# Attention and routed feed-forward on one core: nine idle products instead of eleven, the last spread's halves swapped, some 35 table entries set otherwise

## The chip, the cores and the metric

The kernel runs on 1 core of one Trainium2 chip. The metric is the device time of one execution in microseconds (us), as the median of the runs timed. A core has five engines with an instruction queue each: PE (TensorE, matmuls; PEld is its loading of weights), DVE (VectorE), ACT (ScalarE), POOL (GpSimd) and SP (SyncE, which here only issues DMAs). They run beside one another and wait for each other by semaphores. L723 is line 723 of the kernel before; in the changed kernel the same line stands some 10 to 30 lines further down.

## The reference

Eight batches of S = 3136 tokens, D = 256, scores from a 64-wide `z` of which one array is both query and key. Attention with a squared ReLU in place of a softmax, a product with `u`, then a routed feed-forward for the 128 tokens of each batch with the largest gate score:

```python
scores = (1.0 / S) * np.matmul(z, z.transpose(0, 2, 1))      # symmetric
out = u * np.matmul(np.maximum(scores, 0.0) ** 2, v)
# routed part, per batch b, x = out
top = 128 tokens with the largest x[b] @ w_gate
ye = np.maximum(x[b, top] @ w1, 0.0) @ w2
out[b, top] += sigmoid(score)[:, None] * ye
```

## The kernel before, in words

**Tiles.** The query tokens of a batch come in 7 chunks: five of 512, one of 256, one of 320. For a chunk the 24.5 key tiles of 128 tokens come as 12 pairs and a single half tile (`Vr`), so 13 slots a chunk, 91 a batch, 728 in all. Slots are counted from 0 in each batch. A slot adds its keys' part to the chunk's four PSUM accumulators (`acc`). As the score matrix is symmetric, a block of squared scores that an earlier chunk has computed is written to DRAM (`squares<-aT`) and fetched back (`qk<-squares`): such a slot is "old" and needs no score products.

**A new slot.** PE computes the scores in three products of a high and a low part (`sc<-Z,ZH`, `sc<-Zl,ZH`, `sc<-Z,ZL`, L588; each part is two instructions, one for each half of the rows). There is one score buffer, so the next slot's scores wait until ACT has read it: `a<-sc` is the ReLU (L593). Then ACT takes the square's rounded part, `hi<-a` (L602); the full square `a<-a` is made on ACT (L609) or DVE (L613); the rest `lo<-a,hi` by DVE or POOL (both L694). PE then does 16 instructions with `hi` and 8 with `lo` (`acc<-hi,V`, `acc<-lo,V`, L723). DVE transposes the square for the DRAM copy (`aT<-a`, L656). An old slot has only `hi<-qk` (ACT, L551) and `lo<-qk,hi` (L694). Inputs are split in the same way: `ZH`, `Z`, `V` are casts (L183), `ZL`, `Zl` and V's low part differences (L184).

**Order.** The program is written in a fixed order; each engine runs its own part of it in that order. In slot k the scores of slot k+3 are issued in the middle of slot k's products (`more_scores`). Loads and casts of later data stand in a table of due slots (`plan`), and are issued ahead of a slot's products. The steps of choosing tokens and of the feed-forward are queues of small tasks, woven in one at a time. Which engine does a step is decided by a running account of each engine's work (`busy`, `spend`), unless the table `PICK` has an entry for that slot: `pick(kind, k, default)` (L485) reads `PICK[kind]` at 0 for the first batch, 1 for the six in the middle, 2 for the last. Kinds are `sq` (True: the square on ACT), `lo` (True: the difference on DVE), `tl` (True: a slot's transposes behind its difference), `ne` and `fa` (whether a slot takes a routing task).

**A chunk's end.** `finish_early` (L806) scales two accumulators by ACT (`x<-acc`, L813); `finish` (L817) adds the other two and multiplies by `u` on DVE (`acc<-acc,x` L826, `ut<-acc,ut` L827, half 1 ahead of half 0), DVE transposes to the output's layout (`x<-ut`, L836), POOL multiplies by the gate's weights (`ut<-x,w_run`, L845) and DVE adds up (`gate<-ut`, L854). For the last chunk of the last batch the gate score is a product on PE instead: `spread` (L914) takes half 0 and then half 1 of `ut`, two instructions each.

**The beginning.** `warm(11)` (L1716) issues eleven products of a tile of zeros while the first `z` is on its way; `start` (L1718) then writes the first three slots' steps out by hand.

Of the kernel before, what the change touches and what calls it, by code (L numbers as in the profile page):

```python
# [18 lines left out]
P = 128  # L19
# [10 lines left out]
BITS = 4  # L30
INT_MIN = -(1 << 31)
PICK = {
    "fa": {
        1: {19: False},
        2: {28: False, 30: False, 32: False},
    },
# [4 lines left out]
    },  # L41
    "ne": {
        0: {15: False, 17: True},
        1: {4: True, 13: True, 40: True, 41: False, 42: True, 65: False, 70: False, 71: True, 79: True, 83: False},
    },
# [4 lines left out]
    },  # L50
    "tl": {
        0: {4: True, 8: True, 10: True, 15: True, 50: True},
        1: {6: True, 7: True, 8: True, 26: True, 31: True, 46: True, 56: True},
        2: {0: True, 8: True, 9: False},
    },
}
VH = [0, 0, 0, 0, 0, 0, 0, 1, 0, 0, 1, 0, 1]
VP = [0, 0, 0, 0, 0, 0, -1, 0, 1, 1, 0, 0, -1]
VD = [1, 0, 0, 0, 0, 0, 0, 0, 0, 0, 0, 0, 0]
# [62 lines left out]
def attention_then_routed_ffn(ctx: ExitStack, tc: tile.TileContext, zt, ut, v, wg, w1, w2, cst, cst16, keys, outs, at, cap):  # L122
# [58 lines left out]
    def split(src, hi, lo, hi_on=None, lo_on=None):  # L181

        (hi_on or nc.scalar.copy)(hi, src)  # L183
        (lo_on or nc.vector.tensor_tensor)(lo, src, hi.bitcast(F32), op=ALU.subtract)  # L184
# [161 lines left out]
    def prep_z(b, i, of=None, on=None, hi_on=None):  # L346

        of = i if of is None else of
        a, n = part(i)
        o = a - part(of)[0]  # L350
        on = on or (nc.gpsimd.tensor_tensor if b else None)
        if i < WHOLE:
            for q in range(2):
                src = of_tokens(staged["z", b, of][:, o : o + CH], q)
                split(src, in_pairs(ZH, i, q), in_pairs(ZL, i, q), hi_on, lo_on=on)
            spend(act=0.1, pool=1.8 if b else 0.0)
            return
        m = min(n, NJ * P - a)
        src = staged["z", b, of][:, o : o + m].rearrange("p (f t a) -> p f t a", f=GT, a=Q)
        split(src, by_rows(ZHe, a, m), by_rows(ZLe, a, m), hi_on, lo_on=on)  # L360
        if m < n:
            single = slice(a + m - WIDE, a + n - WIDE)
            split(staged["z", b, of][:, o + m : o + n], ZHe[:, single], ZLe[:, single], lo_on=on)
        spend(pool=0.65 + 0.0017 * n if b else 0.0)
# [9 lines left out]
    def bring_z(b, c):  # L374

        c0, w = CHUNKS[c]
        t, tl = (const.tile([P, CH], F32R, name=name, tag=name, bufs=2)[:, within(c)] for name in ("Z", "Zl"))
        Z[b, c] = t, tl
        if c < WHOLE:
            st = staged.pop(("m", b, c)) if b or c else staged["z", 0, 0]  # L380
            on_dve = not (b or c) or busy["pool"] + 1.2 > busy["dve"] + 0.6
            split(st, t, tl, lo_on=nc.vector.tensor_tensor if on_dve else nc.gpsimd.tensor_tensor)
            spend(act=0.6, **{"dve" if on_dve else "pool": 0.6 if on_dve else 1.2})
            return
        m = min(w, NJ * P - c0)
        for z, to in ((ZHe, t), (ZLe, tl)):
            nc.scalar.copy(to[:, :m].rearrange("p (f t a) -> p f t a", f=GT, a=Q), by_rows(z, c0, m).bitcast(F32))
            if m < w:
                nc.scalar.copy(to[:, m:], z[:, c0 - WIDE + m : c0 - WIDE + w].bitcast(F32))
            spend(act=0.1 + 0.001 * w)  # L390

    def stage_v(b, g, queues=(nc.sync,) * GT):
# [17 lines left out]
    def prep_v(b, g, on=None, hi_on=None):  # L410

        st = staged["v", b, g // 2][:, g % 2 * 2 :]
        n = 2 if 2 * g < NJ else 1
        if n == 2:
            t = vpool.tile([P, 2, NK, 2 * P], F32R, name="V", tag="V")
        else:
            t = vpool.tile([P, 2, NK, P], F32R, name="Vr", tag="Vr", bufs=1)
        src = st[:, :n].rearrange("p a d -> p (a d)").rearrange("p (f h i) -> p h f i", h=NK, i=Q)
        parts_of = [t[:, w].rearrange("p h (f i) -> p h f i", i=Q) for w in range(2)]
        hi_on = hi_on or on  # L420
        lo_on, took = on or nc.gpsimd, {"dve": 1.0} if on else {"pool": 2.3} if hi_on else {"act": 0.6, "pool": 1.3}
        if not on and b == 0 and n == 2 and busy["pool"] + 1.3 > busy["dve"] + 0.6:
            lo_on, took = nc.vector, {"act": 0.6, "dve": 0.6}
        if b and VD[g]:
            lo_on, took = nc.vector, {"act": 0.6, "dve": 0.6}
        if b and VH[g]:
            hi_on = nc.vector
            took = {**took, "act": 0.0, "dve": took.get("dve", 0.0) + 0.6}
        split(src, *parts_of, hi_on and hi_on.tensor_copy, lo_on.tensor_tensor)
        for q in range(n):  # L430
            V[b, 2 * g + q] = t[:, :, :, q * P : (q + 1) * P]
        spend(**took)
# [63 lines left out]
    def spend(act=0.0, dve=0.0, pool=0.0):  # L496
        busy["act"] += act
        busy["dve"] += dve
        busy["pool"] += pool

    fetched = {}
    shared = {}
    stores = []
# [302 lines left out]
    def finish_early(b, c):  # L806

        w = CHUNKS[c][1]
        x = tail.tile([P, CH // Q, NK, Q], F32, name="x", tag="x", bufs=1)
        flat = x.rearrange("p f h r -> p (f h r)")  # L810
        sums = [flat[:, h * w : (h + 1) * w] for h in range(NK)]
        for h in range(NK):
            nc.scalar.mul(sums[h], acc[b, c][h][h], SCALE * SCALE)  # L813
        spend(act=0.3 + 0.0016 * w)
        early[b, c] = x, sums

    def finish(b, c):  # L817
# [72 lines left out]
    def scores_of(b, c, xT):  # L890
# [17 lines left out]
        def spread(h):  # L908
            if not bank:
                bank.append(acc_bank("spread")[:, :w])  # L910
            if more:
                nc.tensor.matmul(bank[0], consts["ones"], row[:, P:], start=True, stop=True)
            else:
                nc.tensor.matmul(bank[0], by_half[h].broadcast_to([P, P]), xT[:, h, :w], start=h == 0, stop=h == NK - 1)  # L914

        def seen(q):
            if q == 0:
# [9 lines left out]
                )  # L927
            spend(act=0.25, dve=0.45)

        return [lambda h=h: spread(h) for h in range(1 if more else NK)], seen  # L930


    def route(b):
# [742 lines left out]
    def more_scores(upto):  # L1676
        nonlocal issued
        while issued <= min(upto, len(slots) - 1):
            scores(issued)
            issued += 1  # L1680

    def settle_scores():
        square_scores()
        for x in lows:
            low(*x)
        lows.clear()
# [30 lines left out]

    def start():  # L1718
        stage_z(0, 0, queues=(nc.sync, nc.scalar))
        warm(11)  # L1720
        first = moe.tile([P, 1], F32, name="g", tag="g", bufs=2)
        nc.scalar.copy(first, idle[0][:, :1])
        stage_z(0, 1, (WHOLE - 1) * CH, CH)
        stage_v(0, 0, (nc.scalar, nc.scalar, nc.sync, nc.sync))
        stage_v(0, 1)
        more_z(0, 2, 1)
        more_z(0, 3, 1)
        low_parts = []
        prep_z(0, 0, None, lambda *x, **how: low_parts.append(lambda: nc.vector.tensor_tensor(*x, **how)), nc.vector.tensor_copy)
        bring_z(0, 0)  # L1730
        for fn in low_parts:
            fn()
        prep_z(0, 1, hi_on=nc.vector.tensor_copy)
        more_scores(0)
        prep_v(0, 0, nc.vector)
        busy["pool"] = 99.0
        settle_scores()
        more_scores(1)
        prep_v(0, 1)
        square_scores()  # L1740
        prep_z(0, 2, 1)
        settle_scores()
        prep_v(0, 2, hi_on=nc.gpsimd)
        more_scores(2)
        settle_scores()
        prep_v(0, 3, hi_on=nc.gpsimd)
        settle_turns()
        busy["pool"] = 0.0
        stage_v(0, 2)
        stage_v(0, 3)  # L1750
# [5 lines left out]
    clock = dve_at = ready = told = 0.0  # L1756
    held_posts = []
    for k, (b, c, js, is_old) in enumerate(slots):
        if k == 0:
            start()  # L1760
        for fn, act, dve in plan.get(k, ()):
            fn()
            spend(act, dve)
        tasks = []
# [38 lines left out]
            for op in f0[0][0][:3]:  # L1803
                op()
        within_end[0] = k % SLOTS >= SLOTS - 2
        mix(k, [op for ops, _ in tasks for op in ops], lambda: more_scores(k + LEAD))
        settle_turns()
        if len(js) == 1 and c == WHOLE:
            lows[0][-1]()
# [92 lines left out]
```

## Time and profile before

| | |
|---|---|
| timed, median of 3 runs | 2007.01 us (2005.39 to 2007.15) |
| the profiled execution's own time | 2004.37 us |
| its span, from first to last record | 2002.6 us |
| TensorE clock granted, mean | 0.998 |
| busy, share of the span | PE 99%, PEld 87%, ACT 75%, DVE 73%, POOL 64% |

How to read it: PE's share of the span is close to all of it, and PE is on the chain that ended last for 93% of its length. So the time is the sum of PE's instructions and of the pieces in which PE waits or its products run further apart than they could. The other engines have a quarter of their time free over the whole, but not everywhere: in the first 50 us ACT and DVE are nearly full. The rows below are of single places.

### The profile page before, as it was taken

Reading aid. Unit: us, or ns where it says so; the run is one execution under the profiler, and the core shown is the slowest. Engines: PE = TensorE matmul, PEld = TensorE weight load, DVE = VectorE, ACT = ScalarE, POOL = GpSimd, SP = SyncE. Lnnn points to the kernel's source line nnn. Section 1 sums busy time; section 2 is a strip of 40 time slices with the busy share of each in tenths; the row PEclk is TensorE's granted clock in tenths of the full one; section 3 lists DMA queues with packets and bytes.
Section 4 is the critical chain, followed back from the end, with each engine's and each line's share of the span. In section 5 each row is a group of like instructions: output and inputs, shape, how many; then the busy total and the mean of one; then the engine's idle time right before and its main releaser. Section 6 shows DMA issues by size and latency. Waiting matters only on the chain.

```text
span 2002.6 us, 51589 instructions
## 1 busy us (share of the span) xinstructions
PE 1981.1 (99%) x19969; PEld 1732.7 (87%) x19969; DVE 1464.4 (73%) x2719; ACT 1495.6 (75%) x2036; POOL 1289.9 (64%) x719
## 2 busy tenths in 40 slices
PE   9999999999999999999999999999999999999998
PEld 6788989899888998889988899888988889878787
DVE  8866688855898568874688746887478864876775
ACT  8786688766887578866798757887588776877653
POOL 4665468657776577755787467865677657775642
PEclk9999999999999999999999999999999999999999
DMA  6788768896678967788677886779867787667852
GB/s 196 224 248 229 227 192 241 237 259 193 199 220 237 241 195 213 216 233 242 185 226 213 235 227 201 221 204 241 237 203 221 200 206 218 199 186 188 230 152 90
DMA packets 450869, 426.96 MB, mean 213 GB/s; under 512 B 136576, under 2 KB 377792, under 8 KB 447808
## 3 DMA queue, kind: packets, MB, share of 16 engines
q1 hardware_dynamic: 449488, 421.18, 74.1%
q8 instruction: 156, 2.56, 0.6%
q0 software_dynamic: 768, 2.10, 0.3%
q14 instruction: 89, 0.73, 0.1%
q10 hardware_dynamic: 368, 0.39, 0.1%
HBM read 248.94 MB, written 174.60 MB: 211 GB/s over the span
## 4 chain that ended last, share of the span: by engine, by line
PE 93%; DMA 2%; ACT 2%; issue 1%; DVE 1%; SPq 0%; POOL 0%; POOLq 0%; ACTq 0%; DVEq 0%
PE acc L723 79%; PE sc L588 10%; PE h L1494 1%; PE sc L571 1%; ACT a L593 1%; DMA qk<-squares 1%; PE y L1550 1%; DMA vst<-in_v 1%; DMA wl<-w1l_there 1%; ACT hi L602 0%; POOL lo L694 0%; PE idle L1716 0%; DVE lo L694 0%; ACT x L813 0%; ACT hi L551 0%
## 5 line engine op out<-in xcount | busy, mean ns | idle before, releaser
L723 PE MATMUL acc<-hi,V 64*128 64x512 f32 (+2 forms) x10752 | 1238.2, 361 | 1.7 <-DVE ut L827 1.3
L723 PEld LDWEIGHTS acc<-hi,V 64*128 64x128 f32 x10752 | 976.3, 184 | 125.6 <-issue 5.5
L694 POOL TENSOR_TENSOR lo<-a,hi 128x1024 fp32r<-128x1024 f32 (+2 forms) x243 | 548.8, 2265 | 330.1 <-ACT a L609 236.6
L723 PE MATMUL acc<-lo,V 64*128 64x512 f32 (+2 forms) x5376 | 693.7, 360 | 2.5 <-POOL lo L694 2.1
L723 PEld LDWEIGHTS acc<-lo,V 64*128 64x128 f32 x5376 | 500.3, 184 | 63.2 <-POOL lo L694 6.2
L593 ACT ACTIVATE a<-sc 128x1024 f32<-128x1024 f32 (+2 forms) x345 | 327.0, 948 | 208.7 <-PE sc L588 196.5
L656 DVE STREAM_TRANSPOSE aT<-a 128x512 f32<-128x512 f32 (+1 forms) x494 | 315.8, 679 | 108.4 <-ACT a L609 100.6
L694 POOL TENSOR_TENSOR lo<-qk,hi 128x1024 fp32r<-128x1024 f32 (+2 forms) x156 | 309.3, 1991 | 101.4 <-ACT hi L551 56.0
L551 ACT CAST hi<-qk 128x1024 fp32r<-128x1024 f32 (+2 forms) x327 | 278.6, 855 | 123.0 <-PE acc L723 83.8
L602 ACT ACTIVATE hi<-a 128x1024 fp32r<-128x1024 f32 (+2 forms) x345 | 339.9, 985 | 24.7 <-PE acc L723 5.8
L609 ACT ACTIVATE a<-a 128x1024 f32<-128x1024 f32 (+1 forms) x280 | 279.2, 997 | 8.2
L694 DVE TENSOR_TENSOR lo<-qk,hi 128x1024 fp32r<-128x1024 f32 (+2 forms) x171 | 235.1, 1387 | 60.0 <-ACT hi L551 54.9
L694 DVE TENSOR_TENSOR lo<-a,hi 128x1024 fp32r<-128x1024 f32 (+1 forms) x102 | 133.2, 1306 | 54.5 <-ACT a L609 43.8
L184 POOL TENSOR_TENSOR V<-vst,V 128x512 fp32r<-128x512 f32 x85 | 138.4, 1634 | 48.9 <-ACT V L183 43.5
L845 POOL TENSOR_TENSOR ut<-x,w_run 128x1024 f32<-128x1024 f32 (+2 forms) x52 | 126.0, 2424 | 28.5 <-DVE x L836 17.0
L613 DVE TENSOR_TENSOR a<-a 128x1024 f32<-128x1024 f32 (+1 forms) x65 | 89.7, 1381 | 44.6 <-ACT hi L602 35.8
L826 DVE SCALAR_TENSOR_TENSOR acc<-acc,x 128x512 f32<-128x512 f32 (+2 forms) x112 | 70.0, 625 | 52.5 <-PE acc L723 47.6
L184 POOL TENSOR_TENSOR ZL<-zst,ZH 64x256 fp32r<-64x256 f32 x70 | 64.9, 927 | 64.5 <-ACT ZH L183 45.6
L588 PE MATMUL sc<-Z,ZH 64*128 64x512 f32 x480 | 96.1, 384 | 9.5 <-ACT a L593 9.5
L813 ACT ACTIVATE x<-acc 128x512 f32<-128x512 f32 (+2 forms) x112 | 54.6, 540 | 56.7 <-PE acc L723 50.0
L588 PE MATMUL sc<-Zl,ZH 64*128 64x512 f32 x480 | 93.1, 372 | 0.0
L588 PE MATMUL sc<-Z,ZL 64*128 64x512 f32 x480 | 92.9, 371 | 0.0
(231 smaller groups left out, 1815.0 us busy)
## 6 DMA issues: line engine op xcount, KB each, us to landing
squares<-aT SPq DMA_DIRECT2D x160, 512.0 KB, 3.4
qk<-squares SPq DMA_DIRECT2D x320, 256.0 KB, 5.4
squares_narrow<-aT SPq DMA_DIRECT2D x320, 128.0 KB, 4.6
qk<-squares_narrow SPq DMA_DIRECT2D x80, 512.0 KB, 4.6
out<-x SPq DMA_DIRECT2D x162, 128.0 KB, 3.1
ut<-in_ut SPq DMA_DIRECT2D x40, 512.0 KB, 6.2
vst<-in_v SPq DMA_DIRECT2D x158, 128.0 KB, 3.6
zmv<-in_zt SPq DMA_DIRECT2D x78, 128.0 KB, 3.3
```

Source lines behind the costliest of these rows:

```text
L184: (lo_on or nc.vector.tensor_tensor)(lo, src, hi.bitcast(F32), op=ALU.subtract)
L551: nc.scalar.copy(by(hi), src)
L588: nc.tensor.matmul(ps[:, q, :w], stationary(high, js[0] // 2, q), mov[m][rows], start=i == 0, stop=i == 2)
L593: nc.scalar.activation(a, ps[:, :, :w], AF.Relu)
L602: nc.scalar.activation(pieces[0][0](hi), pieces[0][1], AF.Square)
L609: nc.scalar.activation(a, a, AF.Square)
L613: square = lambda: nc.vector.tensor_tensor(a, a, a, op=ALU.mult)
L656: nc.vector.transpose(to, a[:, q].rearrange("p (m t a) -> p m t a", m=GT, a=Q))
L694: on.tensor_tensor(view(lo), src, view(hi).bitcast(F32), op=ALU.subtract)
L723: nc.tensor.matmul(bank[g][h][:, cols[g]], V[b, j][rows, i, h], mov[rows], start=(b, c, g, h) not in opened, stop=len(js) == 1 and n == 2,)
L826: nc.vector.scalar_tensor_tensor(rest, rest, SCALE * SCALE, sums[h], op0=ALU.mult, op1=ALU.add)
L845: nc.gpsimd.tensor_tensor(wx, runs, consts["wg_run"].rearrange("p (o r) -> p o r", o=1).broadcast_to([P, NB, RUN]), op=ALU.mult,)
```

## The change

Apart from the tables there are five edits: `warm(WARM)` with `WARM = 9`; the halves of the last spread in reverse order; a kind `xd` by which `finish_early` runs on DVE (one slot of batch 0); a list `ZD` by which the large cast of one prepared part of `z` goes from ACT to DVE in batches 1 to 7; and a kind `pv`, by which a slot's planned casts are issued behind the scores of slot k+3 instead of ahead of the slot's products (slot 3 of batch 0; its other entry is the default). The lists `V0`, `Z0` and `BD` hold zeros only and change nothing, and `bz` has one entry in the last batch. The rest are entries of the old kinds.

```diff
-        0: {2: True, 4: True, 5: True, 7: False, 8: True, ...           # PICK["sq"]
+        0: {1: True, 2: True, 4: True, 5: True, 7: False, 8: True, ...  # PICK["sq"]
...
+    "pv": {
+        0: {3: True},
+        1: {89: False},
+    },
...
+    "xd": {
+        0: {11: True},
+    },
 }
+WARM = 9
...
+ZD = [0, 0, 0, 0, 0, 0, 1, 0]
...
+        zd = ZD[i] if b else Z0[i]
+        if zd and not hi_on:
+            hi_on = (None, nc.vector.tensor_copy, nc.gpsimd.tensor_copy)[zd]
...
+        on_dve = pick("xd", slot_at[0], False)
...
         for h in range(NK):
-            nc.scalar.mul(sums[h], acc[b, c][h][h], SCALE * SCALE)
-        spend(act=0.3 + 0.0016 * w)
+            if on_dve:
+                nc.vector.tensor_scalar(sums[h], acc[b, c][h][h], SCALE * SCALE, None, op0=ALU.mult)
+            else:
+                nc.scalar.mul(sums[h], acc[b, c][h][h], SCALE * SCALE)
+        spend(**{"dve" if on_dve else "act": 0.3 + 0.0016 * w})
...
-                nc.tensor.matmul(bank[0], by_half[h].broadcast_to([P, P]), xT[:, h, :w], start=h == 0, stop=h == NK - 1)
+                nc.tensor.matmul(bank[0], by_half[h].broadcast_to([P, P]), xT[:, h, :w], start=h == NK - 1, stop=h == 0)
...
-        return [lambda h=h: spread(h) for h in range(1 if more else NK)], seen
+        return [lambda h=h: spread(h) for h in reversed(range(1 if more else NK))], seen
...
+    def go_on(k, behind):
+        more_scores(k + LEAD)
+        for fn, act, dve in behind:
+            fn()
+            spend(act, dve)
...
-        warm(11)
+        warm(WARM)
...
         for fn, act, dve in plan.get(k, ()):
+            if act > 0.5 and pick("pv", k, False):
+                behind.append((fn, act, dve))
+                continue
             fn()
             spend(act, dve)
...
-        mix(k, [op for ops, _ in tasks for op in ops], lambda: more_scores(k + LEAD))
+        mix(k, [op for ops, _ in tasks for op in ops], lambda: go_on(k, behind))
```

On PE nothing moves but the idle products and the spread. Three places of the other engines follow. The first is ACT at the beginning, from the first ReLU on. Before:

```order
L593 ACTIVATE a<-sc 128x1024
L602 ACTIVATE hi<-a 128x1024
L593 ACTIVATE a<-sc 128x1024
L602 ACTIVATE hi<-a 128x1024
L183 CAST V<-vst 128x512
L183 CAST ZH<-qk 64x4x2x32 x2
L593 ACTIVATE a<-sc 128x1024
L602 ACTIVATE hi<-a 128x1024
L609 ACTIVATE a<-a 128x1024
L593 ACTIVATE a<-sc 128x1024
L602 ACTIVATE hi<-a 128x1024
L609 ACTIVATE a<-a 128x1024
```

And in the changed kernel, from the same ReLU:

```order
L616 ACTIVATE a<-sc 128x1024
L625 ACTIVATE hi<-a 128x1024
L616 ACTIVATE a<-sc 128x1024
L625 ACTIVATE hi<-a 128x1024
L632 ACTIVATE a<-a 128x1024
L198 CAST V<-vst 128x512
L198 CAST ZH<-qk 64x4x2x32 x2
L616 ACTIVATE a<-sc 128x1024
L625 ACTIVATE hi<-a 128x1024
L632 ACTIVATE a<-a 128x1024
L616 ACTIVATE a<-sc 128x1024
L625 ACTIVATE hi<-a 128x1024
```

Slot 1's square now stands on ACT ahead of the casts of V and ZH and of slot 2's ReLU; slot 3's square has left ACT for DVE.

The second place is DVE in chunk 1 of batch 0, where chunk 0's output is transposed (`x<-ut`) between slots' squares. Before:

```order
L836 STREAM_TRANSPOSE x<-ut 128x16x32
L613 TENSOR_TENSOR a<-a 128x1024
L656 STREAM_TRANSPOSE aT<-a 128x4x128 x2
L694 TENSOR_TENSOR lo<-a,hi 128x1024
L836 STREAM_TRANSPOSE x<-ut 128x16x32
L656 STREAM_TRANSPOSE aT<-a 128x4x128 x2
L854 TENSOR_REDUCE gate<-ut 128x16
```

And in the changed kernel:

```order
L863 STREAM_TRANSPOSE x<-ut 128x16x32
L679 STREAM_TRANSPOSE aT<-a 128x4x128 x2
L717 TENSOR_TENSOR lo<-a,hi 128x1024
L863 STREAM_TRANSPOSE x<-ut 128x16x32
L636 TENSOR_TENSOR a<-a 128x1024
L679 STREAM_TRANSPOSE aT<-a 128x4x128 x2
L881 TENSOR_REDUCE gate<-ut 128x16
```

The square has moved from ahead of the transposes, the difference and the second `x<-ut` to behind them.

The third place is DVE at the beginning of chunk 5 in batches 1 to 6, between the feed-forward's last two instructions (`y`) and chunk 4's finish. Before:

```order
L1558 SCALAR_TENSOR_TENSOR y<-y,g,xe 128x256
L1558 SCALAR_TENSOR_TENSOR y<-y,g 128x256
L826 SCALAR_TENSOR_TENSOR acc<-acc,x 128x512
L827 TENSOR_TENSOR ut<-acc,ut 128x512
L826 SCALAR_TENSOR_TENSOR acc<-acc,x 128x512
```

And in the changed kernel:

```order
L1585 SCALAR_TENSOR_TENSOR y<-y,g,xe 128x256
L1585 SCALAR_TENSOR_TENSOR y<-y,g 128x256
L717 TENSOR_TENSOR lo<-qk,hi 128x2x256
L853 SCALAR_TENSOR_TENSOR acc<-acc,x 128x512
L854 TENSOR_TENSOR ut<-acc,ut 128x512
L853 SCALAR_TENSOR_TENSOR acc<-acc,x 128x512
```

The first old slot's difference (slot 65) has come from POOL, where it was the first of three such behind the indirect DMA that writes `y` out.

## Rows read from the trace of the kernel before

**Rows 1.** Page, part 1: busy time of each engine, share of the span, instructions.

```profile
PE 1981.1 (99%) x19969; PEld 1732.7 (87%) x19969; DVE 1464.4 (73%) x2719; ACT 1495.6 (75%) x2036; POOL 1289.9 (64%) x719
```

**Rows 2.** Waits of PE: line, what it waited for, us in total, times, longest.

```profile
PE sc L588 <- ACT a L593: 9.5, 12, 1.1
PE acc L723 <- POOL lo L694: 2.1, 3, 0.8
```

**Rows 3.** Windows: stretch, length, busy PE, PEld, DVE, ACT, POOL, PEclk, DMA share, GB/s.

```profile
10.00:20.00 10.00, 9.56 (x72) 7.81 (x74) 9.90 (x13) 9.77 (x14) 3.00 (x3) 0.83 0.28 85
20.00:50.00 30.00, 29.24 (x252) 22.61 (x250) 27.55 (x32) 29.33 (x39) 20.66 (x12) 1.00 0.77 237
```

**Rows 4.** Timeline of PE, beginning: start, length, engine, line, operation, count, [idle before <-releaser].

```profile
1.20 4.88 PE L1716 MATMUL idle<-zero 128*128 128x512 bf16 x11 [1.20 <-DVE zero L1713]
...
6.82 0.40 PE L588 MATMUL sc<-Z,ZL 64*128 64x512 f32 x2
...
10.44 0.79 PE L588 MATMUL sc<-Z,ZH 64*128 64x512 f32 x2 [1.12 <-ACT a L593]
...
13.97 0.40 PE L588 MATMUL sc<-Z,ZH 64*128 64x512 f32 x2
...
29.50 0.50 PE L588 MATMUL sc<-Z,ZH 64*128 64x512 f32 x2 [0.74 <-ACT a L593]
```

**Rows 5.** Timelines of DVE (first row) and ACT, beginning.

```profile
5.37 0.86 DVE L1729 TENSOR_TENSOR ZL<-zst,ZH 64x256 fp32r<-64x256 f32 x2
...
7.29 1.02 ACT L593 ACTIVATE a<-sc 128x1024 f32<-128x1024 f32 x1 [2.56 <-PE sc L588]
...
26.10 1.06 ACT L609 ACTIVATE a<-a 128x1024 f32<-128x1024 f32 x1
...
27.57 0.83 ACT L183 CAST ZH<-qk 64x256 fp32r<-64x256 f32 x2
```

**Rows 6.** Timeline of ACT and PE at the end of chunk 0 of batch 0.

```profile
53.83 1.09 ACT L813 ACTIVATE x<-acc 128x512 f32<-128x512 f32 x2 [0.45 <-PE acc L723]
...
58.98 0.49 PE L588 MATMUL sc<-Z,ZH 64*128 64x512 f32 x2 [0.70 <-ACT a L593]
```

**Rows 7.** Timelines of DVE, POOL and PE in chunk 1 of batch 0.

```profile
75.61 3.24 DVE L613 TENSOR_TENSOR a<-a 128x1024 f32<-128x1024 f32 x1 [0.83 <-ACT hi L602]
...
81.21 0.70 DVE L836 STREAM_TRANSPOSE x<-ut 128x512 f32<-128x512 f32 x1
...
81.99 2.40 POOL L845 TENSOR_TENSOR ut<-x,w_run 128x1024 f32<-128x1024 f32 x1 [4.23 <-DVE x L836]
...
86.79 1.21 PE L723 MATMUL acc<-lo,V 64*128 64x512 f32 x8 [0.82 <-POOL lo L694]
```

**Rows 8.** Timelines of ACT, DVE, POOL and PE, beginning of chunk 5 of batch 2.

```profile
695.08 0.62 ACT L551 CAST hi<-qk 128x512 fp32r<-128x512 f32 x1 [1.12 <-PE acc L723]
...
702.24 0.70 DVE L826 SCALAR_TENSOR_TENSOR acc<-acc,x 128x512 f32<-128x512 f32 x1 [2.47 <-PE acc L723]
...
701.10 3.81 POOL L694 TENSOR_TENSOR lo<-qk,hi 128x512 fp32r<-128x512 f32 x3
...
703.73 0.50 PE L723 MATMUL acc<-lo,V 64*128 64x256 f32 x4
...
704.54 0.39 PE L723 MATMUL acc<-lo,V 64*128 64x256 f32 x4
```

**Rows 9.** Timelines of DVE and PE at the last spread.

```profile
1975.56 0.49 DVE L827 TENSOR_TENSOR ut<-acc,ut 128x320 f32<-128x320 f32 x1
...
1976.15 1.31 PE L914 MATMUL spread<-ut,w_col 128*128 128x320 f32 x4 [1.05 <-issue]
```

**Rows 10.** Timelines of DVE and ACT in chunk 1 of batch 2.

```profile
562.50 1.31 DVE L656 STREAM_TRANSPOSE aT<-a 128x512 f32<-128x512 f32 x2
...
565.42 1.03 ACT L593 ACTIVATE a<-sc 128x1024 f32<-128x1024 f32 x1 [0.22 <-PE sc L588]
```

**Rows 11.** Timeline of PE at the boundary between batches 1 and 2.

```profile
500.69 0.50 PE L588 MATMUL sc<-Z,ZH 64*128 64x512 f32 x2 [0.86 <-ACT a L593]
```

More of the change, by code (lines that the diff above doesn't have):

```diff
@@ L32 @@
 PICK = {
+    "bz": {
+        2: {52: False},
+    },
     "fa": {
-        1: {19: False},
+        1: {14: False, 19: False},
         2: {28: False, 30: False, 32: False},
@@ L43 @@
         0: {15: False, 17: True},
-        1: {4: True, 13: True, 40: True, 41: False, 42: True, 65: False, 70: False, 71: True, 79: True, 83: False},
+        1: {4: True, 13: True, 14: True, 40: True, 41: False, 42: True, 65: False, 70: False, 71: True, 79: True, 83: False},
+    },
+    "pv": {
+        0: {3: True},
+        1: {89: False},
     },
     "sq": {
[1 row of a table removed]
[1 row of a table added]
         1: {1: False, 3: False, 6: False, 17: True, 48: False, 62: False, 74: True},
[1 row of a table removed]
[1 row of a table added]
     },
     "tl": {
-        0: {4: True, 8: True, 10: True, 15: True, 50: True},
-        1: {6: True, 7: True, 8: True, 26: True, 31: True, 46: True, 56: True},
-        2: {0: True, 8: True, 9: False},
-    },
-}
[3 rows of a table added]
+    },
+    "xd": {
+        0: {11: True},
+    },
+}
+WARM = 9
+V0 = [0, 0, 0, 0, 0, 0, 0, 0, 0, 0, 0, 0, 0]
+Z0 = [0, 0, 0, 0, 0, 0, 0, 0]
+ZD = [0, 0, 0, 0, 0, 0, 1, 0]
+BD = [0, 0, 0, 0, 0, 0, 0, 0]
 VH = [0, 0, 0, 0, 0, 0, 0, 1, 0, 0, 1, 0, 1]
@@ L380, in bring_z @@
             st = staged.pop(("m", b, c)) if b or c else staged["z", 0, 0]
-            on_dve = not (b or c) or busy["pool"] + 1.2 > busy["dve"] + 0.6
-            split(st, t, tl, lo_on=nc.vector.tensor_tensor if on_dve else nc.gpsimd.tensor_tensor)
+            on_dve = not (b or c) or pick("bz", (b * NCH + c) * SLOTS, busy["pool"] + 1.2 > busy["dve"] + 0.6)
+            split(st, t, tl, (None, nc.vector.tensor_copy, nc.gpsimd.tensor_copy)[BD[c] if b else 0], lo_on=nc.vector.tensor_tensor if on_dve else nc.gpsimd.tensor_tensor)
             spend(act=0.6, **{"dve" if on_dve else "pool": 0.6 if on_dve else 1.2})
@@ L386, in bring_z @@
         for z, to in ((ZHe, t), (ZLe, tl)):
-            nc.scalar.copy(to[:, :m].rearrange("p (f t a) -> p f t a", f=GT, a=Q), by_rows(z, c0, m).bitcast(F32))
+            copy = (nc.scalar.copy, nc.vector.tensor_copy, nc.gpsimd.tensor_copy)[BD[c] if 0 < b else 0]
+            copy(to[:, :m].rearrange("p (f t a) -> p f t a", f=GT, a=Q), by_rows(z, c0, m).bitcast(F32))
             if m < w:
-                nc.scalar.copy(to[:, m:], z[:, c0 - WIDE + m : c0 - WIDE + w].bitcast(F32))
+                copy(to[:, m:], z[:, c0 - WIDE + m : c0 - WIDE + w].bitcast(F32))
             spend(act=0.1 + 0.001 * w)
@@ L425, in prep_v @@
             lo_on, took = nc.vector, {"act": 0.6, "dve": 0.6}
-        if b and VH[g]:
-            hi_on = nc.vector
-            took = {**took, "act": 0.0, "dve": took.get("dve", 0.0) + 0.6}
+        vh = VH[g] if b else V0[g]
+        if vh and not hi_on:
+            hi_on = (None, nc.vector, nc.gpsimd)[vh]
+            took = {**took, "act": 0.0}
+            eng, us = (None, ("dve", 0.6), ("pool", 1.0))[vh]
+            took[eng] = took.get(eng, 0.0) + us
         split(src, *parts_of, hi_on and hi_on.tensor_copy, lo_on.tensor_tensor)
@@ L499, in spend @@
         busy["pool"] += pool
+    slot_at = [0]
     fetched = {}
@@ L1758, in attention_then_routed_ffn @@
     for k, (b, c, js, is_old) in enumerate(slots):
+        slot_at[0] = k
         if k == 0:
             start()
+        behind = []
         for fn, act, dve in plan.get(k, ()):
+            if act > 0.5 and pick("pv", k, False):
+                behind.append((fn, act, dve))
+                continue
             fn()
```

13 rows, old and new, of the table PICK are left out of this document.

## The prediction

> **What bounds the kernel now.** First the busy times: PE is busy for 1981.1 of 2002.6 us, DVE, ACT and POOL for 64 to 75% [rows 1]. So at most 2002.6 - 1981.1 = 21.5 us of the span is without a matmul, and a change that adds and removes none but two idle products can win only such pieces, or pieces in which the products run further apart than they could. Then the waits of PE: 9.5 us in 12 waits of new scores for ACT's ReLU, 2.1 us in three waits for a difference from POOL [rows 2]. Then the timeline at each of these, and at the end, where PE waits 1.05 us ahead of the last spread [rows 9]. Seven of the twelve score waits stand at the boundaries of batches, like the 0.86 us at 500.69 [rows 11]; the order of ACT's steps there is the same in both kernels, so they stay, some 6 us. What the change can reach are the waits of the first 90 us, the spread, and a stretch at the beginning of chunk 5 in which PE hardly waits by the records but is late.
>
> **The change part by part.**
>
> *Two idle products fewer.* Eleven take 4.88 us, so each 4.88/11 = 0.44 us at most; two fewer let PE begin the scores up to 0.9 us earlier [rows 4]. But the third score product needs ZL, whose two halves DVE ends at 5.37 + 0.86 = 6.23; it began at 6.82 [rows 4, 5]. From there it may begin at about 6.3 or 6.4, so ACT's first ReLU, now at 7.29, comes 0.45 us earlier, not 0.9. Everything of the first two slots hangs on that ReLU: -0.45 at this point.
>
> *ACT's order in the first slots.* Slot 1's square goes to ACT, ahead of V's and ZH's casts and slot 2's ReLU: 1.06 us, by the square at 26.10 [rows 5]. The scores of slot 3, at 13.97 without a wait [rows 4], then come at 13.97 - 0.45 + 1.0, about 14.45: 0.5 later than now. Given back: slot 3's square leaves ACT (another 1.06), and the two casts of ZH at 27.57, which stood ahead of the ReLU that slot 7's scores wait for, now stand behind it (0.83). Those scores waited 0.74 us and began at 29.50 [rows 4, 5]; replayed in the new order they begin at about 28.8. Between 20 and 50 us ACT is busy for 29.33 of 30 us [rows 3], so what is won on PE shrinks again as PE comes up with ACT: I take -0.5 for the two parts together. The ends: 0 (ACT gives it all back) and -1.6 (0.85 of idle products and 0.74 of wait both stay won). DVE gives up one square and takes one in this stretch, which is level.
>
> *Chunk 0's scaling to DVE.* `x<-acc` took ACT 1.09 us at 53.83, between two slots' ReLUs, and slot 9 of the new chunk waited 0.70 us for its ReLU at 58.98 [rows 6]. Without it ACT is 1.09 ahead, more than the wait. On DVE the two instructions cost a similar time, and a difference or square that stands behind them becomes later by about 1 us. Ends 0 and -0.70; I take the middle, -0.37, because the records do not show which of the two steps then ends last.
>
> *The second `x<-ut` earlier.* It began at 81.21, behind a square of 3.24 us at 75.61 (one on ACT takes 1.06 [rows 5]) and its successors; POOL waited 4.23 us for it, multiplied for 2.40 us, and the difference behind that product made PE wait 0.82 us [rows 7]. Moved ahead of the square, `x<-ut` ends 3 to 4 us earlier, so POOL's product does; the square's own difference comes later, but no more than that. Ends 0 and -0.82; I take -0.8, because the cover is four times the wait. What is late next is the next score's ReLU, level with PE.
>
> *Chunk 5's first difference to DVE.* In batch 2 POOL does three in 3.81 us from 701.10, 1.27 each, behind the indirect DMA of the feed-forward. DVE is idle for 2.47 us to 702.24, and the first one's `hi` has been there since 695.08 + 0.62 [rows 8]. So DVE can do it at once, before its next step can begin, and POOL's next two are not behind it. What that is worth on PE: the four products with a difference at 703.73 run for 0.50 us against 0.39 for the same four at 704.54 [rows 8], a sign of products that come one by one as data is ready. Two or three such pieces are 0.1 to 0.23 us a batch, six batches: ends 0 and -1.4, taken -0.9 (0.15 each). More is hardly there, since the second and third difference stay on POOL at the same 1.27 us.
>
> *The spread's halves.* DVE finishes half 1 first; half 0 begins at 1975.56 and ends at 1976.05, and PE's first spread product, which needs half 0, starts at 1976.15 and the four take 1.31 us [rows 9]. With half 1 first, PE may start once half 1 is done, 0.49 us sooner, and its first two products (half of 1.31 is 0.65) end at about 1976.3, when half 0 is there: all four end 0.49 us sooner. What follows on PE stands behind them. Ends 0 and -0.65; taken -0.5.
>
> *The rest.* The large cast of one `z` part goes from ACT to DVE in seven batches, some differences change sides, and in the middle batches three DVE steps of chunk 1 stand ahead of the counting chain. DVE is idle 27% of the span and POOL 36% [rows 1], and none of PE's waits above stands there. Taken 0; if that cover is gone, a cast costs 0.83/2 = 0.42 us by the two of rows 5, and seven of them 2.9 us; a difference that changes sides costs POOL what it gives DVE.
>
> Sum: -0.5 - 0.37 - 0.8 - 0.9 - 0.5 = -3.1 us. The profiled execution took 2004.37 us (1.8 outside its span), so it would take 2001.25. The median of the runs shown, 2007.01, lies 2.64 above that execution; the same step from there gives **2003.9 us**.
>
> **A page and the rows.** The granted clock fell to 0.83 between 10 and 20 us [rows 3]; the pair of score products at 10.44 took 0.79 us, where at 29.50 it took 0.50 [rows 4]. So TensorE went from its upper level (2.4 GHz) to its lower (1.2 GHz) and back in that stretch, after a ReLU wait of 1.12 us. The Trainium skill ("TensorE: Matmul & The Clock Gate", What's actually happening) says that the throttled state is the default and that activity releases it. The rows agree that the level moves with what the engine has done; by that rule fewer idle products make the release at the beginning less sure, which is the third rival's mechanism.
>
> **Rivals.** *All waits go wholly, at the bounds.* -1.6 - 0.70 - 0.82 - 1.4 - 0.65 = -5.2, so 2001.8 us. For it: the covers are longer than the waits in three of the five. Against: behind each PE wait there is a next limit on ACT in the first 60 us.
>
> *Only the beginning and the spread count.* -0.5 and -0.5, so 2006.0 us: the other waits come back at the next slot because ACT or DVE is the limit of those stretches. For it: ACT's 29.33 of 30 us [rows 3]. Against: POOL's 4.23 us of waiting for `x<-ut` has a plain cause that goes.
>
> *The clock rises later.* The pieces at the lower level cost 0.17 of 10 us, 1.7 us [rows 3]. With two idle products fewer, a second such stretch, or one longer by as much, follows: -3.1 + 1.7, so 2005.6 us. Against: PE begins its real products sooner, by about as much as the idle ones end sooner.
>
> *Slower: DVE's late transposes in the middle batches.* In chunk 1 a difference, two transposes and the gate's sum, which waits for POOL's product, now stand ahead of the counting chain. Transposes that were done at 562.50 + 1.31 = 563.81 free a buffer for the ReLU at 565.42 [rows 10]: 1.6 us of room, and some 0.7 more with the split of `z` that leaves DVE there (an estimate, half of the transposes' time). From a delay of over 2.3 us on, ACT's ReLU is late, then PE's scores. Three steps of some 1.2 us each (an estimate by the transposes' 1.31) are 3.6 us, 1.3 too late, in each of six batches: -3.1 + 7.7 = +4.6, so 2011.6 us. Against: the steps are moved, not added, and the chain behind them is itself short.
>
> **How the numbers follow.** A measurement of this kernel tells a change from none from about 0.2% on, 4.0 us: faster means below 2003.0, slower above 2011.0. The forecast has a chance of 50%, with its own range 2002 to 2005.5, a quarter of it below 2003.0; all waits at their bounds 22%, faster; only the beginning and the spread 15%, the same; the clock 7%, the same; the late transposes 6%, slower. Faster: 0.125 + 0.22, rounded 0.35; slower 0.06; the same 0.59. The range goes from 2000.2 (the second case's 2001.8 less 1.6, by which the lowest run lies under the median) to 2007.5 (the third case's 2006.0 and as much again), which leaves out the slower case and the far ends.
>
> **What the changed profile would show.** Right: the first ReLU near 6.85; scores of slot 7 before 29.0 without a wait for ACT; no wait near 58 and none for POOL's difference near 86, with `ut<-x,w_run` starting before 79; at chunk 5's beginning a difference on DVE between `y` and `acc`, and PE's fours at 0.40; the spread's wait down by about 0.5; and PE's waits for a ReLU down from 9.5 to about 8 us in all. Wrong: a later start of chunk 1 than now, a wait of scores for ACT in the slots around 565 in batch 2, or a second stretch of low clock before 20 us. And if waits go where I said while the time stays, they have come back as products further apart, which PE's busy time in the windows of 50 us would show.

## The result, and the profile after

The changed kernel is slower: 2024.28 us (median of 6 runs, 2017.32 to 2026.9) against 2006.03 us (6 runs), ratio 1.0083, 95% interval [1.0064, 1.0102]. The forecast was 2003.9. The runs of the changed kernel lie 10 us apart, those of the kernel before less than 2 (3 to 5 in the larger sets taken beside the experiments). The profiled execution is the lowest of the six (2017.32 us, span 2015.5), so it shows some of the loss, not all.

The page's busy times and PE's waits, the latter as line, waited for, us in total, times, longest:

```profile
PE 1986.1 (99%) x19967; PEld 1738.2 (86%) x19967; DVE 1486.4 (74%) x2735; ACT 1493.7 (74%) x2026; POOL 1273.3 (63%) x713
```

```profile
PE sc L611 <- ACT a L616: 8.6, 12, 1.1
PE acc L746 <- POOL lo L717: 7.3, 10, 0.8
PE acc L746 <- DVE hi L653: 2.2, 1, 2.2
PE acc L746 <- DVE lo L717: 1.8, 2, 1.5
```

Against [rows 1] PE has 5 us more busy time though it has less to do: its products run further apart, in part at the lower clock (below). Against [rows 2] the waits for a ReLU fell by 0.9 us (the forecast was about 1.5); those for a POOL difference rose from 2.1 to 7.3, and the two larger kinds for DVE are new. Lined up by the starts of ScalarE's ReLUs, the changed kernel is 1.1 us ahead at 100 us, then loses 1.3 to 1.4 us at the end of chunk 0 in each of the six middle batches, and once, at the end of chunk 1 of batch 5, 5.7 us.

The steady loss is at the end of chunk 0. First the kernel before there in batch 3 (timelines of DVE, POOL, POOL), then the changed kernel (DVE, POOL, DVE, POOL, POOL, PE):

```profile
771.00 0.73 DVE L183 CAST V<-vst 128x512 fp32r<-128x512 f32 x1
...
771.81 4.00 POOL L184 TENSOR_TENSOR V<-vst,V 128x512 fp32r<-128x512 f32 x2 [0.36 <-DVE V L183]
...
775.78 2.53 POOL L694 TENSOR_TENSOR lo<-a,hi 128x1024 fp32r<-128x1024 f32 x1
```

```profile
762.52 2.21 DVE L198 CAST ZHe<-zst 128x256 fp32r<-128x256 f32 x1
...
759.80 4.77 POOL L717 TENSOR_TENSOR lo<-a,hi 128x1024 fp32r<-128x1024 f32 x2
...
774.68 0.41 DVE L198 CAST V<-vst 128x512 fp32r<-128x512 f32 x1
...
775.17 4.01 POOL L199 TENSOR_TENSOR V<-vst,V 128x512 fp32r<-128x512 f32 x2 [3.42 <-DVE V L198]
...
779.13 2.51 POOL L717 TENSOR_TENSOR lo<-a,hi 128x1024 fp32r<-128x1024 f32 x1
...
781.70 1.21 PE L746 MATMUL acc<-lo,V 64*128 64x512 f32 x8 [0.84 <-POOL lo L717]
```

The moved cast takes 2.21 us on DVE and ends at 764.73, just after POOL's two differences (764.57). DVE's cast of V, further down its row, is 3.7 us later, 0.9 of it because the batch began later; POOL waits 3.42 us for it, its difference starts 3.35 us later, and PE waits.

The single loss is at the end of chunk 1 of batch 5 (POOL, DVE, DVE, then three rows of PE):

```profile
1298.30 7.13 POOL L717 TENSOR_TENSOR lo<-a,hi 128x1024 fp32r<-128x1024 f32 x3
...
1300.66 2.42 DVE L1047 TENSOR_TENSOR base<-place,flip 32x1 int32<-32x1 int32 x1
...
1317.16 2.87 DVE L717 TENSOR_TENSOR lo<-vst,hi 128x512 fp32r<-128x512 f32 x1
...
1320.09 1.19 PE L746 MATMUL acc<-lo,V 64*128 64x512 f32 x8 [1.50 <-DVE lo L717]
...
1325.07 0.39 PE L746 MATMUL acc<-hi,Vr 64*128 64x256 f32 x2 [2.18 <-DVE hi L653]
...
1327.41 0.63 PE L611 MATMUL sc<-Z,ZH 64*128 64x512 f32 x2
```

A step on 32 numbers (`base`) takes 2.42 us beside POOL, later a difference 2.87; PE waits twice, and then runs a while at its lower clock (granted 0.66 between 1325 and 1330 us; a pair of score products takes 0.63 us, against 0.40 in [rows 4]).

The first 50 us answer to [rows 3 to 5] (PE, windows, ACT):

```profile
1.19 4.02 PE L1749 MATMUL idle<-zero 128*128 128x512 bf16 x9 [1.19 <-DVE zero L1746]
...
14.58 0.80 PE L611 MATMUL sc<-Z,ZH 64*128 64x512 f32 x2 [0.26 <-ACT a L616]
...
29.36 0.39 PE L611 MATMUL sc<-Z,ZH 64*128 64x512 f32 x2
...
30.53 1.20 PE L746 MATMUL acc<-lo,V 64*128 64x512 f32 x8 [0.33 <-DVE lo L717]
```

```profile
10.00:20.00 10.00, 9.63 (x60) 7.32 (x62) 8.37 (x12) 9.73 (x14) 3.04 (x3) 0.71 0.29 85
20.00:50.00 30.00, 29.29 (x253) 22.99 (x252) 29.77 (x32) 28.68 (x37) 19.75 (x11) 1.00 0.72 222
```

```profile
6.95 1.02 ACT L616 ACTIVATE a<-sc 128x1024 f32<-128x1024 f32 x1 [2.10 <-PE sc L611]
```

Slot 7's scores no longer wait for ACT, but begin at 29.36, not at 28.8, and right behind them PE waits for DVE. Between 20 and 50 us DVE is busy for 29.77 of 30 us. This counts the time that a step is held up, too. PE's wait at 30.53 is for the DVE difference below. It runs beside one that POOL began at 27.00, and takes 3.20 us where another takes 1.18 (at 78.72):

```profile
27.28 3.20 DVE L717 TENSOR_TENSOR lo<-a,hi 128x1024 fp32r<-128x1024 f32 x1
```

Chunk 1 starts later than in the kernel before: its first ReLU stands at 52.34, not at 51.26.

The other forecast places answer to [rows 6 to 9] (PE near 58 us; DVE, POOL and PE near 86; DVE and PE in chunk 5; DVE and PE at the spread):

```profile
59.79 0.50 PE L611 MATMUL sc<-Z,ZH 64*128 64x512 f32 x2 [0.43 <-ACT a L616]
...
80.45 1.18 DVE L636 TENSOR_TENSOR a<-a 128x1024 f32<-128x1024 f32 x1
...
80.61 3.29 POOL L872 TENSOR_TENSOR ut<-x,w_run 128x1024 f32<-128x1024 f32 x1 [2.17 <-DVE x L863]
...
86.60 1.07 PE L746 MATMUL acc<-lo,V 64*128 64x512 f32 x8
...
701.11 0.68 DVE L717 TENSOR_TENSOR lo<-qk,hi 128x512 fp32r<-128x512 f32 x1
...
704.99 0.50 PE L746 MATMUL acc<-lo,V 64*128 64x256 f32 x4
...
1989.37 0.49 DVE L854 TENSOR_TENSOR ut<-acc,ut 128x320 f32<-128x320 f32 x1
...
1989.03 1.69 PE L941 MATMUL spread<-ut,w_col 128*128 128x320 f32 x4
```

The wait near 58 shrank from 0.70 to 0.43, that for POOL near 86 is gone, the spread starts before half 0 is done, and in chunk 5 one group of four still takes 0.50 us.

So several of the signs that the prediction named for being right are missed: a wait is left near 58, slot 7's scores begin behind 29.0, POOL's product at 80.61 and not before 79, and a group of four still takes 0.50 us. Of its three signs of being wrong, two are there: chunk 1 starts later, and the clock is low for longer before 20 us (granted 0.71 between 10 and 20 us, against 0.83 in [rows 3]). The third, a wait of scores for ACT around 565, is not.

### The profile page after: what moved, and what is told of

It reads as the page before. It is cut to its first block, busy times and chain, and to the rows that moved or that the text cites. A ratio compares the mean times of both kernels' runs of the same rounds, so it can differ in the third digit from the quotient of the medians.

```text
span 2015.5 us, 51607 instructions
## 1 busy us (share of the span) xinstructions
PE 1986.1 (99%) x19967; PEld 1738.2 (86%) x19967; DVE 1486.4 (74%) x2735; ACT 1493.7 (74%) x2026; POOL 1273.3 (63%) x713
## 4 chain that ended last, share of the span: by engine, by line
PE 81%; DVE 5%; issue 3%; DMA 3%; POOL 3%; ACT 2%; SPq 2%; POOLq 0%; DVEq 0%; ACTq 0%
PE acc L746 69%; PE sc L611 8%; POOL lo L717 2%; DVE aT L679 1%; SPq L423 1%; PE h L1521 1%; ACT a L616 1%; DVE a L636 1%; PE y L1577 1%; DMA qk<-squares_narrow 1%; PE sc L594 1%; ACT hi L625 1%; DVE lo L717 1%; POOL V L199 1%; DMA wl<-w1l_there 0%
## 5 line engine op out<-in xcount | busy, mean ns | idle before, releaser
L717 POOL TENSOR_TENSOR lo<-a,hi 128x1024 fp32r<-128x1024 f32 (+1 forms) x235 | 528.2, 2252 | 323.8 <-ACT a L632 221.2
L717 POOL TENSOR_TENSOR lo<-qk,hi 128x1024 fp32r<-128x1024 f32 (+2 forms) x151 | 303.4, 2014 | 105.5 <-ACT hi L574 63.6
L717 DVE TENSOR_TENSOR lo<-a,hi 128x1024 fp32r<-128x1024 f32 (+1 forms) x110 | 150.1, 1365 | 51.5 <-ACT a L632 44.1
L636 DVE TENSOR_TENSOR a<-a 128x1024 f32<-128x1024 f32 (+1 forms) x66 | 94.2, 1428 | 35.5 <-ACT hi L625 35.1
```

Of the source, the lines that this page charges most:

```text
L636: square = lambda: nc.vector.tensor_tensor(a, a, a, op=ALU.mult)
L717: on.tensor_tensor(view(lo), src, view(hi).bitcast(F32), op=ALU.subtract)
```

## Experiments

**Cast or table: two by two.** Theory A blames the cast, theory B the middle batches' entries. `ZD` zero puts the cast back on ScalarE; `PICK` column 1 as before takes the entries out: eight of the 28 in which the two tables differ, one of them (`pv`, slot 89) the default.

```diff
-ZD = [0, 0, 0, 0, 0, 0, 1, 0]      # first and fourth run
+ZD = [0, 0, 0, 0, 0, 0, 0, 0]
+        if b and i == 6 and not hi_on:      # second run, in the kernel before
+            hi_on = nc.vector.tensor_copy
-        1: {14: False, 19: False},     # third and fourth run: all kinds, as before
+        1: {19: False},
```

Cast back: 

> The changed kernel with only the ZHe cast of batches 1 to 7 back on ScalarE. Theory A (the cast on VectorE, 2.2 us there against 0.4 on ScalarE, makes VectorE late in chunk 0, so that POOL's difference is late and PE waits about 1.3 us in each of six or seven batches, and leaves too little room at the end of chunk 1, where single stalls of some 5 us come up): 2003 to 2007 us, the single-run scatter of 10 us goes too. Theory B (the entries for slots 14 to 17 of the middle batches delay VectorE's transposes): 2018 to 2025 us, as the changed kernel.

Measured 2015.76 us (2007.35 to 2020.37), ratio 1.005 [1.0032, 1.0067].

Cast alone: 

> The kernel before with only that cast moved to VectorE. Theory A: 2014 to 2022 us, with a wait of PE for POOL's difference of about 0.8 us at the end of chunk 0 of batches 1 to 6. Theory B: 2006 us, as before, at most 2 us more.

Measured 2013.34 us (2013.02 to 2013.61), 1.0042 [1.0029, 1.0055].

Middle entries out: 

> The changed kernel with the middle six batches' table entries as before, the cast still on VectorE. Theory A: 2012 to 2020 us; the single stalls at the end of chunk 1 may go, since less stands on VectorE there, the 1.3 us a batch stay. Theory B: 2003 to 2006 us.

Measured 2011.55 us, 1.0032 [1.002, 1.0043].

Both out: 

> The changed kernel with the cast back on ScalarE and the middle batches' entries as before: what is left of the change is the start, the first and the last batch and the spread. Both theories: 2004 to 2006 us; by the two traces up to 100 us (1.1 us ahead) and after 1950 us (0.9 us ahead), about 2 us under the kernel before. Against the first run it tells what the middle entries alone are worth: theory A forecasts within 2 us of it, theory B some 15 us less.

Measured 2004.08 us, 0.9996 [0.9987, 1.0005]; the kernel before 2004.89 beside these four.

Neither theory alone holds: both parts cost. The cast costs 8.5 us on the kernel before and 7.5 on the changed one (2011.55 - 2004.08); the middle entries 11.7 (2015.76 - 2004.08). 2004.08 + 7.5 + 11.7 = 2023.3, near the 2024.28. The cast's loss is steady, the entries' scatters.

**Why the cast costs.** Grouped by form (count: shortest/median/longest in ns, first and last start), the cast of the changed kernel, and the same values made by a sum over one element:

```diff
+        if b and i == 6 and not hi_on:
+            hi_on = by_sum    # nc.vector.tensor_reduce over an axis of 1
```

> The kernel before with the ZHe cast on VectorE in batches 1 to 7, written as a sum over an axis of one element. Theory D (VectorE's plain cast is held until POOL's running instruction ends: 2.2 us in six of seven, 0.28 in one; sums take the same time beside POOL or not): the seven take 0.3 to 0.5 us each, no wait of PE for POOL's difference at the end of chunk 0, 2004 to 2007 us. Rival (any further step on VectorE in chunk 0 makes it late, whatever its form): 2010 to 2014 us, near the 2013.3 of the plain cast.

```profile
L198 DVE CAST ZHe<-zst x7: 276/2204/2216, 270.7 to 1750.9; 128x256 fp32r<-128x256 f32 x7
```

```profile
L350 DVE TENSOR_REDUCE ZHe<-zst x7: 374/376/404, 270.8 to 1739.2; 128x256 fp32r<-128x256 f32 x7
```

Measured 2005.17 us, 1.0001 [0.9993, 1.001]. Six of the seven sums begin where the long casts do, 0.4 us into a difference of POOL; beside the seventh, and beside the one short cast, POOL does nothing. So a further step on DVE in chunk 0 costs nothing; the cast's being held beside POOL is the 8 us. PE's waits for POOL's differences, with the plain cast alone and with the sum (of these five none stands at the end of chunk 0):

```profile
PE acc L725 <- POOL lo L696: 7.9, 11, 0.9
```

```profile
PE acc L731 <- POOL lo L702: 3.1, 5, 0.8
```

The Trainium skill ("SBUF — State Buffer", Who interferes with whom) has the rule: GpSimd shares a pair of ports with VectorE, whichever starts first holds it for its whole instruction and the other waits; casts in a mode that uses both ports contend, and so does a step with two SBUF inputs against a GpSimd step that reads SBUF, while `tensor_reduce` does not. The trace agrees: 0.28 us for the cast without POOL, 2.2 beside it, and 0.37 to 0.40 for the sum. The other side shows, too: POOL's product at 80.61, which begins 0.2 us behind a DVE square of 1.18 us, takes 3.29 us instead of 2.40 [rows 7].

**Which entries, and why by chance.** The three entries of chunk 1 in the kernel before, and the four of chunks 5 and 6:

```diff
+    fa 1: {14: False}    ne 1: {14: True}    tl 1: {17: True}               # chunk 1
+    lo 1: {65: True, 84: False, 86: True, 89: True}                         # chunks 5 and 6
```

> The kernel before with only the three entries of slots 14 and 17 of the middle batches (fa 14, ne 14, tl 17). Theory C (these put a difference, two transposes and the gate's sum ahead of the counting chain in chunk 1, so VectorE ends the chunk with no room, and in some batches PE waits for it by 2 to 5 us): 2010 to 2018 us with a scatter of some us between runs. Rival (the entries of chunks 5 and 6 are what the middle table costs): 2003 to 2007 us.

Measured 2021.83 us (2014.32 to 2026.64), 1.0075 [1.0058, 1.0092].

> The kernel before with only the four lo entries of the middle batches (65, 84, 86, 89). Theory C: within 1.5 us of the kernel before; the 0.9 us that the prediction gave the first difference of chunk 5 is seen inside the chunk as 0.2 to 0.3 us a batch and given back at the batch's end, so nearer 0 than -0.9. Rival: 2010 us or more.

Measured 2004.15 us, 0.9996 [0.9987, 1.0005], the kernel before 2004.53.

So chunk 1's three entries are all of the table's cost. With them alone, two batches in one execution, batch 3 (POOL, DVE) and batch 2 (POOL, DVE, POOL):

```profile
807.71 2.41 POOL L694 TENSOR_TENSOR lo<-a,hi 128x1024 fp32r<-128x1024 f32 x1 [0.82 <-PE sc L588]
...
808.01 2.12 DVE L1020 TENSOR_TENSOR base<-place,flip 32x1 int32<-32x1 int32 x1
```

```profile
560.51 2.41 POOL L694 TENSOR_TENSOR lo<-a,hi 128x1024 fp32r<-128x1024 f32 x1
...
562.87 0.15 DVE L1020 TENSOR_TENSOR base<-place,flip 32x1 int32<-32x1 int32 x1
...
563.09 2.41 POOL L694 TENSOR_TENSOR lo<-a,hi 128x1024 fp32r<-128x1024 f32 x1 [0.17 <-PE sc L588]
```

`base` has two SBUF inputs. In batch 3 it starts 0.3 us after POOL's difference and ends as that ends; in batch 2 it falls between two of them. Over the three profiles with these entries (changed kernel, cast back, entries alone) `base` was held in 1, 4 and 5 of six middle batches, and PE waited for DVE's `hi` at the end of chunk 1 in just those 1, 4 and 5. The waits of the execution with the entries alone:

```profile
PE acc L723 <- DVE hi L630: 9.5, 5, 2.2
```

Lined up by the ReLUs, this execution loses 4.4, 4.7, 0.9, 3.1 and 4.7 us at these five places and nothing in batch 2: 17.8 of the 17.9 us by which it lies above the kernel before's median. Over the 5 us behind three of the five waits the granted clock is 0.66, so a part of the loss is the clock's. In the kernel before it is held in all six (1.45 to 2.20 us), a slot earlier in the chain, and there is room. Now what makes it wait is taken away, not the entries:

```diff
-            nc.vector.tensor_tensor(base, k, flip, op=ALU.bitwise_xor)
+            nc.vector.tensor_scalar(base, k, flip, None, op0=ALU.bitwise_xor)
```

> The kernel with the chunk 1 entries alone (2021.8 us, 2014 to 2027) with one more edit: the step base of place and flip (32x1) takes flip as a scalar of a tensor_scalar, not as a second tensor. Theory F (a VectorE step with two SBUF inputs is held to the end of POOL's running difference; with the entries this step starts at the same moment as POOL's difference, takes 0.15 or 2.1 us by chance, and after 2.1 the chunk's end is late and PE waits): base takes 0.2 us in every batch, 2004 to 2007 us, scatter below 4 us. Rival (the entries make chunk 1 too full in any case, or it is the held difference lo of vst that decides): 2012 us or more, with the scatter.

```profile
L1020 DVE TENSOR_SCALAR base<-place,flip x8: 201/202/213, 313.8 to 1862.2; 32x1 int32<-32x1 int32 x6, 98x1 int32<-98x1 int32 x1, 96x1 int32<-96x1 int32 x1
```

Measured 2004.88 us (2003.88 to 2006.73), 1.0000 [0.9991, 1.0009]: with these entries, one instruction of 32 numbers a batch was worth 17 us, and the scatter went with it.

**The whole change with both steps rewritten** (the sum and the scalar form above):

> The changed kernel whole, with the ZHe cast on VectorE written as a sum over one element, and base by tensor_scalar. If the two held steps are all that made the change slower: 2003 to 2006 us, without the 10 us scatter. If something else of the change costs too: above 2007 us.

Measured 2003.25 us (2001.03 to 2005.53), 0.9989 [0.998, 0.9998]. With the two held steps gone the change is on the faster side; what else in it costs is smaller.

**The beginning.** Eleven idle products in the changed kernel without cast and entries:

```diff
-WARM = 9
+WARM = 11
```

> The changed kernel with cast and middle entries as before (2004.1 us) and eleven idle products instead of nine. Theory E (with nine, TensorE runs longer at its lower clock after 8 us: granted 0.71 to 0.77 between 10 and 20 us in the four profiles with nine, 0.83 and 1.00 in the two with eleven): a granted clock of 0.83 or more there and 2002 to 2003.5 us. Rival (idle products only stand in the way of the scores): 2004.5 to 2005 us.

Measured 2004.18 us, 0.9999 [0.9991, 1.0008], against 2004.08 with nine: theory E is not borne out in the time, though the granted clock between 10 and 20 us is lower with nine: 0.71 to 0.78 in the five profiles with nine, 0.83 or 1.00 in the nine with eleven. Two windows of this run's profile:

```profile
10.00:20.00 10.00, 8.76 (x62) 6.91 (x64) 8.36 (x11) 9.77 (x14) 2.58 (x3) 0.83 0.28 84
20.00:50.00 30.00, 29.18 (x250) 22.68 (x248) 29.77 (x33) 28.66 (x37) 19.92 (x11) 1.00 0.72 220
```

DVE's 29.77 us are there with eleven too: they come from the order of the first slots. Two more runs follow: the late edits of batch 0 and the spread without the new beginning, and the rewritten change with the old beginning:

```diff
-    sq 0: {1: True, ...}   lo 0: {10: False, ...}   tl 0: {4: False, 5: True, ...}   pv 0: {3: True}   WARM = 9
+    these as in the kernel before; slots 11 to 37 as changed; WARM = 11
+    (first of the two runs: cast, middle and last batch as in the kernel before, too)
```

> The kernel before with the change's entries for slots 11 to 37 of batch 0 (chunk 0's scaling on VectorE, the second x<-ut ahead of the square) and the spread's halves swapped; start, cast and middle batches as before. The prediction's terms for these are -0.37, -0.8 and -0.5, so 1.7 us under the kernel before (2004.5): 2002.8 us. Rival (they come back in the slots behind): 2004.5 us. In the profile: no wait of PE near 58 and 86 us, the spread's wait about 0.5 us.

Measured 2002.08 us, 0.9987 [0.9978, 0.9996], the kernel before 2004.88. PE's wait near 58 us is the one below; there is none for POOL near 86:

```profile
58.29 0.50 PE L604 MATMUL sc<-Z,ZH 64*128 64x512 f32 x2 [0.44 <-ACT a L609]
```

> The changed kernel with both remedies (2003.25 us) and the beginning as before: eleven idle products, and ScalarE's order of the first slots as before (without the entries for slots 1 to 10 of batch 0). Theory G (ScalarE's new order at the beginning, slot 1's square ahead of slot 2's ReLU, costs about 1.5 us that are not given back; the idle products hardly count): 2001 to 2002.5 us, and PE at the third score pair's position as in the kernel before at 14 and 57 us. Rival (the beginning is worth the -0.5 us of the prediction): 2003.5 to 2004 us.

Measured 2000.94 us (1999.26 to 2003.2), 0.9982 [0.9973, 0.9991], the kernel before 2004.99. It beats both kernels and lies a little below theory G's range. Its window from 20 to 50 us, with DVE at 27.54 us again:

```profile
20.00:50.00 30.00, 29.18 (x250) 22.52 (x248) 27.54 (x32) 29.27 (x40) 20.65 (x12) 1.00 0.78 239
```

The traces show the same by themselves. From the first ReLU to the first one of chunk 1, the eight profiles with the old order of the first slots take 43.9 to 44.0 us, the six with the new order 45.3 to 46.2, and the least of these is the one with eleven idle products. So the order alone costs 1.3 us by then. Which of its entries does it, no run separates.

## Why the prediction was wrong

**The step that failed** is "The rest", taken at 0 because DVE is idle for 27% of the span and POOL for 36%. By the runs its two costly parts are worth 7.5 and 11.7 us in the changed kernel. The first is the cast: its price was taken from ScalarE, 0.42 us at most in each of seven batches. On DVE beside POOL it takes 2.2 us, and in chunk 0 that lateness is passed on by V's cast and POOL's difference. The second is the three steps of chunk 1 (next paragraph). What was missing was not DVE's mean load but what POOL does at that moment. The hint stood in the prediction's own rows: the square of 3.24 us in [rows 7] began 0.3 us into a difference of POOL and took 1.18 us in the changed kernel, behind the second `x<-ut`, where it began ahead of POOL's product; it was read as the square's own length.

**The slower rival** named the right place: a difference, transposes and the gate's sum ahead of the counting chain in chunk 1 of the middle batches. It was given 6%, and its mechanism was wrong: PE waited for DVE's own steps, not for a late ReLU. The chain's start met POOL's difference, `base` was held for some 2.1 us, later often the difference of `vst` (2.9 us instead of 0.68), and PE waited for the half tile. Its price, 1.3 us in each batch, is 1 to 5 us in some: 17 us with the entries alone, 11.7 in the changed kernel.

**The beginning** (-0.5) has the wrong sign. Slot 7's wait went, as replayed, and up to slot 6's ReLU the changed kernel gains 0.8 us. But "DVE gives up one square and takes one" was not level: DVE went from 27.55 us [rows 3] to 29.77 of 30, PE's first waits behind slot 7 are for DVE, one of them for a difference held beside POOL, and by the first ReLU of chunk 1 the 0.8 us gained have turned into 1.4 us lost. In whole runs it is 2003.25 - 2000.94 = 2.3 us by medians; the two ratios' intervals overlap, so the size is not sure, and the sign rests on the traces as well. The clock's rival had its condition (the granted clock fell further) but not its price of 1.7 us: nine or eleven idle products differ by 0.1 us. That the first ReLU came near the forecast 6.85 shows nothing: with eleven idle products it stands anywhere from 6.74 to 7.49 in nine profiles.

**Chunk 0's scaling, the second `x<-ut`, the spread** (-0.37, -0.8, -0.5, together -1.7) hold as a sum: -2.8 us by medians with an interval of -4.4 to -0.8, and the waits at the forecast places went or shrank, that near 58 only to 0.44 where none was forecast. Their single sizes are not shown, since the run moves them together with a few other entries of slots 11 to 37. **Chunk 5's difference** (-0.9): -0.4 us with the other three `lo` entries, interval -2.6 to +1.0; whether anything stays of it is open. Three slips in the prediction's sums, none over 0.07 us, change nothing: 13.97 - 0.45 + 1.0 is 14.52, the middle of 0 and -0.70 is -0.35, and 2004.37 - 3.1 is 2001.27.

## What to carry to other kernels

Before a step goes to VectorE, look at what GpSimd runs at that moment: a cast, or a step with two SBUF inputs, beside a GpSimd tensor operation can cost the rest of that operation, as here: 2.2 us for a cast of 0.28 and 2.1 us for a step of 0.15. The same values can be made by a form that is not held (a sum over one element, a scalar operand in place of a second tensor). A kernel whose runs lie 10 us apart where its neighbours' lie 3 to 5 apart may have such a meeting near its critical path: compare the length of one instruction from batch to batch, not its mean.

## What the runs showed of the hardware that was not expected

A 32x1 step took 0.15 us or up to 2.42 us, and with chunk 1's entries this decided over 1 to 5 us of PE's time in a batch. Written with `flip` as a scalar operand it took 0.20 to 0.21 us in all eight places, though in six of them POOL was in the middle of an instruction.
